# Five shifted copies for VectorE's exponential, column strips for full matmuls, and packed heads, in a fused attention and MLP kernel

## The chip, the cores and the metric

The kernel runs on one core of a Trainium2 chip. Its time is the device time of one launch in microseconds (us). Five engines matter here, named as in the profile: PE (TensorE, matmuls; PEld is its weight load), DVE (VectorE), ACT (ScalarE), POOL (GpSimd) and SP (SyncE, which issues most DMAs). Before the change the median of 3 runs is 805.33 us (805.23 to 805.93).

## The reference, cut to what matters

One input x (2048 tokens by 512, bfloat16) goes through attention with 32 heads of width 16 and through an MLP with two layer norms, two gelus and four weight matrices. A gate for each token mixes the two.

```python
qkv = x @ wqkv                                     # 32 heads, Dh = 16
scores = einsum("bhqd,bhkd->bhqk", q, k) * Dh**-0.5
a = (softmax(scores) @ v) @ wo
h = gelu(layernorm(x) @ w1)                        # quarters of h shifted along the tokens
x1 = x + shifted(h) @ w2
b = x1 + gelu(layernorm(x1) @ w3) @ w4             # w3: 512 x 1792
g = sigmoid((x * gate_w).sum(-1))
out = g * a + (1 - g) * b
```

The softmax needs 32 x 2048 x 2048 exponentials. They are the bulk of the work, and the two engines that make them are ACT and DVE.

## The kernel before

**Units and blocks.** A unit is one chunk of 512 queries (`c`) with four heads (`u`); there are 32 units, worked on one after the other. A unit has 64 blocks: 16 key tiles of 128 (`kt`) by 4 heads (`j`). One block is a score matmul (line 709) that writes 128 keys x 512 queries to PSUM, the exponential, and an attend matmul (line 960) that adds V times the exponentials to the unit's accumulator `acc`. V carries a column of ones, so the sum of the exponentials comes along. The query tile `qT` has two slots: a mask leaves alternate groups of 16 rows at zero in each, so that a head of width 16 fills a row group of 32. Four heads sit in the four row groups of PE and are scored side by side, and the four attend matmuls of one key tile sit in four column groups side by side.

**Two makers of exponentials.** Scores come in slots. A slot has two or three blocks in a `stage` tile, which ACT turns into `pt` with one Exp (line 947). In many slots the third block goes to a tile `dsc` instead, which DVE reads. Four such blocks, of four heads, make a quad. DVE works with the bits of bfloat16 as integers: `dump` (line 873, once for each block) scales the score into exponent and mantissa bits in int16, and four operations over the whole quad (`mantissa` 883, `square` 888, `power` 893, `later` 898) make three terms whose sum approximates the exponential. PE adds each term to `acc` with attend matmuls of its own, so a quad costs PE three attend groups of four.

**The other work.** Projections, MLP matmuls, the gates' products and output tiles are generators (`proj`, `w2_tile`, `w4_tile`, `out_tile`, ...) cut into pieces that go through `bmm` (line 223), one 128 x 128 x 512 matmul at a time, between the scores. A gelu needs another function table on ACT; `gelu_slot` (line 713) then puts gelu matmuls through the score slots, in five places of the run. Where nothing is to be done, `fill` (line 1254) issues a matmul of zeros.

**What sets the order.** The whole program is laid out by a planner inside the kernel when it is built. It holds a time for each engine and an estimated cost for each operation, and picks the next instruction by rank and due time; `RULES` gives each unit its own limits, among them how many blocks DVE may take. Its costs include `MM` (one matmul), `TURN` (what PE loses between kinds of matmul) and the `at[...]` entries, which say when a tile is ready. On the chip the engines run that fixed order and wait for each other by semaphores. SP's queue is in order too: for each unit it copies the sums of exponentials out of `acc` (line 1036), writes their reciprocals to DRAM (1044) and reads them back spread out (1045).

**What the change touches besides.** `q_proj` (line 260) fills both slots of `qT` by one DVE multiplication with `mask` over 128 x 1024. `scale` in `finish_unit` (1048) writes one padded tile `oT` per unit, with 16 of every 32 rows in use; `out_tile` (493) multiplies eight of them per output tile with `wo_pad`. `wants_whole` (643) decides whether a slot gives a block to DVE.

Of the kernel before, what the change touches and what calls it, by code (L numbers as in the profile page):

```python
# [26 lines left out]
SHIFT = 127.0 * 128.0 + 128.0 * log2(0.60404289)  # L27
QUARTER = 32.0 - 3.0 * 128.0
LOWEST = 128.0 - QUARTER


@with_exitstack
def kernel(
# [13 lines left out]
    nc = tc.nc  # L47
# [8 lines left out]
    OB = 8  # L56
# [25 lines left out]
    qpool = ctx.enter_context(tc.tile_pool(name="qpool", bufs=2))  # L82
# [15 lines left out]
    wo_pad = const.tile([P, NU, D], BF16, name="wo_pad")  # L98
# [50 lines left out]
    nc.sync.dma_start(out=gw[:], in_=gate_w.rearrange("(kt p) -> p kt", p=P))  # L149
    for j in range(4):  # L150
        src = A_wo.rearrange("(G j a d) n -> j a d G n", j=4, a=2, d=DH)[j]
        for a in range(2):
            nc.sync.dma_start(
                out=wo_pad[32 * j + 1:32 * j + 1 + DH, :, :].rearrange("d (G a) n -> a d G n", a=2)[a],
                in_=src[a])
# [4 lines left out]
    USUAL = {"NEED": 34, "AHEAD": 16, "HURRY": 14, "DLIM": 1.8, "MANY": 5, "PTS": 4, "CHAINS": 3}  # L160
    RULES = {1: {"NEED": 26, "HURRY": 0, "MANY": 5, "PTS": 6, "CHAINS": 3}, 2: {"NEED": 26, "HURRY": 0, "DLIM": 1.5, "MANY": 4, "PTS": 5}, 4: {"AHEAD": 16, "HURRY": 8}, 6: {"AHEAD": 6, "HURRY": 0, "DLIM": 2.1, "MANY": 4, "CHAINS": 4}, 7: {"MANY": 3, "PTS": 6}, 8: {"NEED": 26, "HURRY": 18, "CHAINS": 3}, 9: {"NEED": 36, "HURRY": 8, "DLIM": 2.1, "MANY": 3, "CHAINS": 5}, 10: {"DLIM": 1.2, "MANY": 5, "CHAINS": 4}, 12: {"NEED": 26, "HURRY": 18, "MANY": 2}, 13: {"HURRY": 8, "PTS": 5}, 14: {"NEED": 28, "AHEAD": 16, "HURRY": 24, "CHAINS": 5}, 15: {"AHEAD": 10, "MANY": 2, "PTS": 5}, 16: {"NEED": 28, "AHEAD": 16, "DLIM": 1.8, "MANY": 2}, 18: {"NEED": 30, "AHEAD": 6, "HURRY": 0, "MANY": 5}, 19: {"NEED": 32, "DLIM": 1.5}, 20: {"AHEAD": 8, "DLIM": 2.1, "MANY": 4, "PTS": 3, "CHAINS": 4}, 21: {"NEED": 32, "AHEAD": 16, "HURRY": 8, "PTS": 5}, 22: {"AHEAD": 8, "HURRY": 18, "MANY": 3, "PTS": 5}, 23: {"NEED": 30, "AHEAD": 12, "HURRY": 14, "DLIM": 2.1, "CHAINS": 4}, 24: {"NEED": 34, "AHEAD": 8, "MANY": 4, "PTS": 5}, 27: {"AHEAD": 10, "DLIM": 1.8, "CHAINS": 4}, 28: {"NEED": 26, "DLIM": 1.5, "MANY": 4}, 29: {"AHEAD": 10, "DLIM": 1.5, "MANY": 5, "CHAINS": 3}, 30: {"NEED": 28, "AHEAD": 10, "DLIM": 1.5, "MANY": 4}, 31: {"NEED": 32, "HURRY": 18, "MANY": 5, "PTS": 6, "CHAINS": 5}}
    MM = 0.2235
    TURN = 0.09
    PE_OUT = 0.43
    WARM = 8
    EARLY = 34
    DUNIT = 1
    MAXD = 16
# [4 lines left out]
    CREDIT = 0.45  # L173
    LATER = 0.4
    GELU, WTWO = 1.0, 1.6
    MOST = 12.0
# [4 lines left out]
    SLACK = 0.3  # L181
    AGE = 2.0
    ARANK = 3
    TANH = 1.5
# [3 lines left out]
    state = {"n": 0, "gen": 0, "young": True, "mm": 0, "kind": "", "t": 0.0, "piece": 0.0,  # L188
# [30 lines left out]

    def bmm(*args, **kwargs):  # L220
        state["mm"] += 1
        state["piece"] += MM
        nc.tensor.matmul(*args, **kwargs)  # L223
# [34 lines left out]
    qTs = {}  # L258

    def q_proj(c, G):  # L260
# [4 lines left out]
        def fn(end):  # L265
            qT = qpool.tile([P, 2, CH], BF16, tag="qT", name="qT")
            qTs[(c, G)] = qT
            nc.vector.tensor_tensor(out=qT[:], in0=ps[:].unsqueeze(1).to_broadcast([P, 2, CH]),
                                    in1=mask[:].unsqueeze(2).to_broadcast([P, 2, CH]), op=ALU.mult)
            at["q", c, G] = end  # L270
# [102 lines left out]
    def gates(c):  # L373
# [3 lines left out]
        for j in range(4):  # L377
# [5 lines left out]
            if j < 3:  # L383
                yield 0.3
# [980 lines left out]
```

## Time and profile before

| | |
|---|---|
| time, median of 3 (range) | 805.33 us (805.23 to 805.93) |
| the profiled execution's span | 803.7 us |
| ACT, PE, DVE busy, share of the span | 98%, 96%, 95% |
| Exp on ACT | 695 instructions, 738.1 us busy |
| score matmuls for ACT, for DVE | 1644, 428 |
| granted TensorE clock | 0.997 |

The profile lists no time of its own execution apart from the span. In it, "xN" is the number of instructions of a group; behind the bar stand the busy time, the mean duration of one, and the engine's idle time just before them with what ended it. Durations of neighbouring instructions overlap by some tens of nanoseconds, so the pitch from start to start is shorter than the duration.

### The profile page before, as it was taken

What the parts mean: (1) busy time and instruction counts of PE and PEld (TensorE: products, weight loads), DVE (VectorE), ACT (ScalarE), POOL (GpSimd) and SP (SyncE); (2) the same over time, 40 slices, a digit from 0 to 9 for tenths busy, and PEclk for the clock granted to TensorE, in tenths of its full rate; (3) what the DMA queues carried; (4) which work ended last, traced back from release to release, by engine and by line L of the source; (5) the groups of instructions that cost most, each with busy time, mean ns of one, the idle gap of its engine ahead of it and who ended that gap; (6) DMA issues with size and microseconds to landing.
All of it is one profiled execution on the core that took longest, in us unless ns stands there. A gap on an engine that the chain in (4) does not pass through costs nothing.

```text
span 803.7 us, 15774 instructions
## 1 busy us (share of the span) xinstructions
PE 773.4 (96%) x6332; PEld 245.8 (31%) x6332; DVE 760.8 (95%) x1237; ACT 787.6 (98%) x734; POOL 19.6 (2%) x46
## 2 busy tenths in 40 slices
PE   9999999999999999999999999999999999999997
PEld 3333333332322323232222233222233233322223
DVE  5799999999889999999999997999999999999995
ACT  6999999999999999999999999999999999999996
POOL 4100000000000000010000000000000000000000
PEclk9999999999999999999999999999999999999998
DMA  8700031230100033001000001001001000000000
GB/s 201 179 15 15 16 67 28 41 42 15 42 1 15 15 106 42 15 1 41 15 14 26 18 15 41 15 3 42 13 14 41 15 6 12 21 21 29 15 15 27
DMA packets 48176, 26.41 MB, mean 33 GB/s; under 512 B 34664, under 2 KB 43624, under 8 KB 48104
## 3 DMA queue, kind: packets, MB, share of 16 engines
q1 hardware_dynamic: 47144, 24.90, 13.0%
q8 instruction: 49, 0.80, 0.4%
q10 hardware_dynamic: 960, 0.52, 0.2%
q14 instruction: 23, 0.19, 0.1%
HBM read 17.04 MB, written 2.35 MB: 24 GB/s over the span
## 4 chain that ended last, share of the span: by engine, by line
ACT 59%; issue 21%; PE 17%; DVE 2%; DVEq 0%; ACTq 0%
ACT pt L947 54%; PE stage L709 5%; PE acc L960 4%; PE ps L223 3%; ACT g2T L925 2%; ACT g2T L928 1%; DVE st L311 1%; ACT L925 1%; PE ps_y L223 1%; PE acc L1259 1%; ACT hT L925 1%; PE ps_v L281 1%; PE ps_k L223 1%; PE warm L1177 0%; PE spare L1262 0%
## 5 line engine op out<-in xcount | busy, mean ns | idle before, releaser
L947 ACT ACTIVATE pt<-stage 128x1024 bf16<-128x1024 f32 (+1 forms) x695 | 738.1, 1236 | 2.6 <-PE stage L709 1.2
L709 PE MATMUL stage<-qT,kT 32*128 32x512 bf16 (+2 forms) x1644 | 270.9, 379 | 22.1 <-ACT pt L947 10.8
L873 DVE TENSOR_SCALAR quad<-dsc 128x512 int16<-128x512 f32 x320 | 213.2, 684 | 13.7 <-PE dsc L709 11.8
L709 PE MATMUL dsc<-qT,kT 32*128 32x512 bf16 x428 | 164.5, 384 | 0.0
L960 PE MATMUL acc<-pt,vp 128*17 128x512 bf16 (+3 forms) x1644 | 157.1, 380 | 1.1 <-ACT pt L947 0.8
L709 PEld LDWEIGHTS <-kT 32*128 32x128 bf16 x2072 | 83.5, 91 | 237.1 <-issue 203.8
L960 PEld LDWEIGHTS <-vp 128*17 128x17 bf16 (+1 forms) x2928 | 60.3, 88 | 131.4 <-issue 119.4
L960 PE MATMUL acc<-quad,vp 128*17 128x512 bf16 x884 | 82.7, 382 | 0.3
L1259 PE MATMUL acc<-wq,zero 128*128 128x512 bf16 x216 | 75.9, 387 | 0.0
L223 PE MATMUL ps<-w,g2T 128*128 128x512 bf16 x224 | 68.4, 384 | 0.8 <-DVE x_sb L433 0.8
L898 DVE TENSOR_SCALAR quad<-quad 128x2048 int16<-128x2048 int16 x80 | 54.2, 679 | 0.3
L223 PE MATMUL ps_y<-xnT,w 128*128 128x512 bf16 x176 | 54.1, 384 | 0.1
L873 DVE TENSOR_SCALAR xT<-dsc 128x512 int16<-128x512 f32 x60 | 40.0, 684 | 0.7 <-PE dsc L709 0.4
L888 DVE TENSOR_TENSOR quad<-quad,quad 128x2048 bf16<-128x2048 bf16 x30 | 36.4, 1213 | 0.3
L883 DVE TENSOR_SCALAR quad<-quad 128x2048 int16<-128x2048 int16 x50 | 34.2, 683 | 0.1
L893 DVE TENSOR_SCALAR quad<-quad 128x2048 int16<-128x2048 int16 x50 | 34.1, 682 | 0.1
L873 DVE TENSOR_SCALAR more<-dsc 128x512 int16<-128x512 f32 x48 | 32.2, 686 | 0.9 <-PE dsc L709 0.2
L1259 PEld LDWEIGHTS <-zero 128*128 128x128 bf16 x216 | 19.1, 96 | 44.8 <-issue 41.6
L223 PEld LDWEIGHTS <-g2T 128*128 128x128 bf16 x224 | 16.9, 97 | 33.1 <-issue 27.5
L723 PE MATMUL stage<-xnT,w 128*128 128x512 bf16 x112 | 25.0, 379 | 0.1
L960 PE MATMUL acc<-more,vp 128*17 128x512 bf16 x248 | 24.3, 382 | 0.0
L1031 DVE COPY accsb<-acc 128x512 f32<-128x512 f32 x31 | 21.2, 684 | 1.6 <-PE acc L960 1.3
(145 smaller groups left out, 682.0 us busy)
## 6 DMA issues: line engine op xcount, KB each, us to landing
bcs<-rec_d SPq DMA_DIRECT2D x31, 256.0 KB
w<-in_B_w_dram SPq DMA_DIRECT2D x2, 1792.0 KB
out_dram<-ot SPq DMA_DIRECT2D x15, 128.0 KB
x_sb<-in_A_x_dram SPq DMA_DIRECT2D x14, 128.0 KB
w<-in_B_w_dram SPq DMA_DIRECT2D x2, 512.0 KB
wkv<-in_A_wqkv_dram SPq DMA_DIRECT2D x1, 512.0 KB
wo_pad<-in_A_wo_dram SPq DMA_DIRECT2D x8, 64.0 KB
xnT<-xn SPq DMA_TRANSPOSE x32
```

Of the source, the lines that this page charges most:

```text
L223: nc.tensor.matmul(*args, **kwargs)
L709: nc.tensor.matmul(out, lhsT=kT[G][32 * j:32 * j + 32, cc, o:o + P], rhs=qTs[(c, G)][32 * j:32 * j + 32, a, lo:hi], start=True, stop=True, ...
L723: nc.tensor.matmul(stages[k][:, i * CH:(i + 1) * CH], lhsT=w[:, kt, m * P:(m + 1) * P], rhs=rhs[:, kt, :], start=(kt == 0), stop=(kt == KT ...
L873: nc.vector.tensor_scalar(out=bits[:, r, :], in0=dsc[:], scalar1=SHIFT, scalar2=LOWEST, op0=ALU.add, op1=ALU.max)
L883: nc.vector.tensor_scalar(out=tiles["once"], in0=bits, scalar1=0x7F, scalar2=0x3F00, op0=ALU.bitwise_and, op1=ALU.bitwise_or)
L888: nc.vector.tensor_tensor(out=tiles["twice"].bitcast(BF16), in0=bits.bitcast(BF16), in1=tiles["once"].bitcast(BF16), op=ALU.mult)
L893: nc.vector.tensor_scalar(out=tiles["once"], in0=bits, scalar1=0x7F80, scalar2=None, op0=ALU.bitwise_and)
L898: nc.vector.tensor_scalar(out=bits, in0=bits, scalar1=QUARTER, scalar2=None, op0=ALU.add)
L925: nc.scalar.activation(out=part, in_=part, func=ACT.Gelu_apprx_tanh)
L947: nc.scalar.activation(out=pt[:, 0:w], in_=stages.pop(k)[:, 0:w], func=ACT.Exp, scale=LN2 / 128.0)
L960: nc.tensor.matmul(accs[n][32 * j:32 * j + M, lo:hi], lhsT=lhsT, rhs=p, start=(kt == 0), stop=(kt == NT - 1), skip_group_check=True, tile_ ...
L1259: nc.tensor.matmul(acc[:], lhsT=zero[:], rhs=wq[:, 0, :], start=False, stop=False, skip_group_check=True)
```

## The change

- **Exponential on DVE.** A quad keeps its four dumps. Instead of three terms out of four operations, DVE makes four copies of the bits, each with a constant added (`STEPS`), and PE sums the five terms. Three more buffers of this kind and freed tiles (`more`, `xT`) hold them.
- **Column strips.** `bmm`, `v_proj`, `gelu_slot` and `fill` issue each full matmul as four of 32 columns of weights, in the four column groups that the attends use. The planner charges `TURN` only between these and the scores. The zero matmuls in `gates` go.
- **Packed heads.** `scale` still writes a padded tile; four DMAs per unit then copy its rows into a tile without gaps that takes two units, so an output tile needs four products with `wo_all` instead of eight. The last two units keep the padded way.
- **Queries by DMA.** From the third query tile on, DVE scales 128 x 512 once, and eight DMAs of 16 rows put the rows into the two slots. The planner takes them as landed 3.5 us later.
- **Slots for DVE alone.** Before the first and after the last gelu slot of a group, `lone_slot` may score up to three blocks that only DVE reads.
- **The planner.** New costs, and `RULES` is set anew for all units.

```diff
-SHIFT = 127.0 * 128.0 + 128.0 * log2(0.60404289)
-QUARTER = 32.0 - 3.0 * 128.0
+STEPS = (-32.0, -57.0, -99.0, -82.0)
+SHIFT = 127.0 * 128.0 - 128.0 * log2(3.95352827)
...
+    wo_rows = A_wo.rearrange("(G j a d) n -> j a d G n", j=4, a=2, d=DH)
     for j in range(4):
         for a in range(2):
+            o = 64 * a + DH * j
+            nc.sync.dma_start(out=wo_all[o:o + DH, :, :], in_=wo_rows[j][a])
...
-    MM = 0.2235
-    TURN = 0.09
+    MM = 0.212
+    TURN = 0.102
+    NARROW = ("full", "attend")
...
+    def strips(out, lhsT, rhs, **kwargs):
+        for j in range(0, P, 32):
+            nc.tensor.matmul(out[j:j + 32, :], lhsT=lhsT[:, j:j + 32], rhs=rhs, tile_position=(0, j), **kwargs)
+
     def bmm(*args, **kwargs):
         state["mm"] += 1
         state["piece"] += MM
-        nc.tensor.matmul(*args, **kwargs)
+        strips(*args, **kwargs)
...
+            both = qpool.tile([P, CH], BF16, tag="both", name="both")
+            nc.vector.tensor_scalar(out=both[:], in0=ps[:], scalar1=QS, scalar2=None, op0=ALU.mult)
+            for o in range(0, P, DH):
+                nc.sync.dma_start(out=qT[o:o + DH, o // DH % 2, :], in_=both[o:o + DH, :])
+            at["q", c, G] = end + 3.5
...
-            bmm(ps[:, 64:CH], lhsT=zero[:], rhs=wq[:, 0, 64:CH], start=True, stop=True)
...
-        for u in range(units):
-            bmm(aps[:], lhsT=oTs[(c, u)][:, j * P:(j + 1) * P], rhs=wo_pad[:, u, :],
-                start=False, stop=(u == units - 1))
+        for G in range(pairs):
+            bmm(aps[:], lhsT=oPs[(c, G)][:, j * P:(j + 1) * P], rhs=wo_all[:, G, :],
+                start=False, stop=(G == pairs - 1))
...
-            t = max(t, done_exp[k - 2], dumped.get(k - 2, 0.0))
+            t = max(t, done_exp[k - 2] + 0.005, dumped.get(k - 2, 0.0) - 0.12)
...
     def scores(start):
         k = len(slots)
+        first, after = gelus and gelus[0][1], state["after"] and not gelus and not ends
+        state["after"] = False
+        if (first and state["before"] or after) and lone_slot(start):
+            state["before"] = not first
+            return
...
+    def lone_slot(start):
...
+        for i in range(3):
+            if i:
+                mine = wants_whole([], start, True)
+            if not mine:
+                break
+            n, kt, j = mine
...
+            score(st[:, i * CH:(i + 1) * CH], n, 4 * kt + j)
+            whole(k, st[:, i * CH:(i + 1) * CH], n, kt, j, begin + (rows[j] - 1) * MM + PE_OUT)
...
-        def mantissa(end):
-            nc.vector.tensor_scalar(out=tiles["once"], in0=bits, scalar1=0x7F, scalar2=0x3F00,
-                                    op0=ALU.bitwise_and, op1=ALU.bitwise_or)
...
-        def square(end):
-            nc.vector.tensor_tensor(out=tiles["twice"].bitcast(BF16), in0=bits.bitcast(BF16), in1=tiles["once"].bitcast(BF16), op=ALU.mult)
...
-        def later(end):
-            nc.vector.tensor_scalar(out=bits, in0=bits, scalar1=QUARTER, scalar2=None, op0=ALU.add)
+        def shifted(end, i):
...
+            base = (0, 0, 0, 1)[i]
...
+            nc.vector.tensor_scalar(out=tiles[to], in0=tiles[base], scalar1=STEPS[i] - (STEPS[0] if base else 0.0), scalar2=None, op0=ALU.add)
...
+            produce(n, kt, heads, tiles[to], end, i == 3, used(to))
...
         def scale(end):
...
+            for j in range(4):
+                nc.sync.dma_start(out=oPs[(c, G)][64 * a + DH * j:64 * a + DH * j + DH, :], in_=oT[32 * j + 1:32 * j + 1 + DH, :])
+            at["o", c, u] = end + 3.0
```

More of the change, by code (lines that the diff above doesn't have):

```diff
@@ L258 @@
     qTs = {}
+    qbufs = [const.tile([P, 2, CH], BF16, name=f"qT{i}") for i in range(2)]
     def q_proj(c, G):
@@ L641, in remaining, with wants_whole @@
         return 4 * NT - place["m"] - sum(4 * kt + j >= place["m"] for kt, j in taken[n])
-    def wants_whole(blocks, now):
+    def wants_whole(blocks, now, alone=False):
         k = len(slots)
-        if k < EARLY or k - quad["last"] < SPACE:
+        if k < EARLY or k - quad["last"] < SPACE and not alone:
             return None
@@ L985, in attend @@
     def attend(start, source):
-        begin = start + (TURN if state["kind"] != "attend" else 0.0)
+        begin = start + (TURN if state["kind"] not in NARROW else 0.0)
         free["pe"] = begin + MM
```

233 lines of the change are left out of this document (152 added, 81 removed).

## The prediction

> **What bounds the kernel now.** I read the page's first part for the load of each engine, then the windows for where an engine rests, then the groups by line and shape, and the timeline for the pitch from one instruction to the next.
>
> ```profile
> PE 773.4 (96%) x6332; PEld 245.8 (31%) x6332; DVE 760.8 (95%) x1237; ACT 787.6 (98%) x734; POOL 19.6 (2%) x46
> ACT 59%; issue 21%; PE 17%; DVE 2%; DVEq 0%; ACTq 0%
> ```
>
> ```profile
> 0.00:50.00 50.00, 47.71 (x331) 17.62 (x331) 35.86 (x87) 43.20 (x48) 13.02 (x41) 1.00 0.63 153
> 100.00:200.00 100.00, 96.32 (x826) 30.14 (x823) 99.16 (x159) 99.89 (x93) 0.00 (x0) 1.00 0.23 39
> 200.00:300.00 100.00, 94.46 (x786) 30.72 (x783) 93.59 (x152) 99.94 (x94) 1.96 (x1) 1.00 0.12 36
> 400.00:500.00 100.00, 96.98 (x783) 30.00 (x781) 94.08 (x146) 99.89 (x92) 0.00 (x0) 1.00 0.08 23
> 700.00:804.00 104.00, 96.83 (x839) 30.66 (x837) 93.58 (x148) 95.78 (x90) 1.26 (x1) 0.98 0.07 21
> ```
>
> In the windows the columns behind the length are PE, PEld, DVE, ACT and POOL. From 100 us on ACT is busy 99.9% until the last window, and the chain that ends last runs mostly over it: a microsecond taken from ACT is a microsecond, as long as PE and DVE keep up. DVE is nearly as full. Its 42.9 us of rest (803.7 - 760.8) lie at the start (14), at the end (10), and 6 each in two windows with a gelu. PE looks full too, but its matmuls overlap and part of them multiply zeros, so its load has to be counted from pitches.
>
> **ACT.**
>
> ```profile
> L947 ACT ACTIVATE pt<-stage 128x1024 bf16<-128x1024 f32 (+1 forms) x695 | 738.1, 1236 | 2.6 <-PE stage L709 1.2 <-PE dsc L709 0.2 <-ACT pt L947 0.2
> L947 ACT ACTIVATE pt<-stage 128x1024 bf16<-128x1024 f32 x465 | 441.7, 1095 | 1.9 <-PE stage L709 1.2 <-PE dsc L709 0.2 <-ACT pt L947 0.2
> L947 ACT ACTIVATE pt<-stage 128x1536 bf16<-128x1536 f32 x230 | 321.5, 1519 | 0.7
> ```
>
> The shapes differ by one block, their means by 424 ns. The 695 instructions hold 465 x 2 + 230 x 3 = 1620 blocks, 686.9 us at 424 ns; the other 51.2 of 738.1 us are 74 ns for each instruction, small waits included. Counted in the changed program, ACT has 485 instructions of two blocks and 202 of three: 1576 blocks in 687 instructions. 1576 x 0.424 + 687 x 0.074 = 719 us, **19.2 us less**. Gelus and table loads are the same in number. The 44 blocks go to DVE (118 quads for 107).
>
> **DVE.**
>
> ```profile
> L873 DVE TENSOR_SCALAR quad<-dsc 128x512 int16<-128x512 f32 x320 | 213.2, 684 | 13.7 <-PE dsc L709 11.8
> L888 DVE TENSOR_TENSOR quad<-quad,quad 128x2048 bf16<-128x2048 bf16 x30 | 36.4, 1213 | 0.3
> L898 DVE TENSOR_SCALAR quad<-quad 128x2048 int16<-128x2048 int16 x80 | 54.2, 679 | 0.3
> L268 DVE TENSOR_TENSOR qT<-ps_q,mask 128x1024 bf16<-128x1024 f32 x15 | 18.2, 1215 | 0.3 <-PE ps_q L223 0.3
> ```
>
> ```profile
> 304.23 1.22 DVE L888 TENSOR_TENSOR quad<-quad,more 128x2048 bf16<-128x2048 bf16 x1
> 305.36 1.28 DVE L873 TENSOR_SCALAR quad<-dsc 128x512 int16<-128x512 f32 x2
> 306.56 0.68 DVE L1031 COPY accsb<-acc 128x512 f32<-128x512 f32 x1
> 307.15 0.68 DVE L893 TENSOR_SCALAR more<-quad 128x2048 int16<-128x2048 int16 x1
> 307.75 0.41 DVE L331 TENSOR_SCALAR xn<-x_sb,mv,rstd 128x512 bf16<-128x512 bf16 x1
> ```
>
> In the timeline the first number is the start. A dump that lasts 684 ns is followed 0.60 us later, an integer operation over a quad too (307.15 to 307.75), `square` 1.13 us later. A quad costs DVE 4 x 0.60 + 3 x 0.60 + 1.13 = 5.33 us before, and 4 x 0.60 + 4 x 0.60 = 4.80 after: a copy is the same kind of instruction as `later` in L898, an added constant over 128x2048 int16. 107 x 5.33 = 570.3, 118 x 4.80 = 566.4: 3.9 us less. 14 query tiles shrink from 1215 ns to a 128x512 operation like the dump (684), 7.4 less. Together **11.3 us less**, for 44 blocks more. Its rest may then be 42.9 - 19.2 + 11.3 = 35 us; the lone slots are put where it rested at a gelu.
>
> **PE.**
>
> ```profile
> 302.14 0.39 PE L1259 MATMUL acc<-wq,zero 128*128 128x512 bf16 x1
> 302.46 0.39 PE L960 MATMUL acc<-quad,vp 128*17 128x512 bf16 x4
> 302.79 0.39 PE L1259 MATMUL acc<-wq,zero 128*128 128x512 bf16 x1
> 304.13 0.39 PE L709 MATMUL stage<-qT,kT 32*128 32x512 bf16 x2
> 304.45 0.39 PE L960 MATMUL acc<-pt,vp 128*17 128x512 bf16 x4
> 304.77 0.39 PE L1259 MATMUL acc<-wq,zero 128*128 128x512 bf16 x1
> ```
>
> ```profile
> 214.87 3.61 PE L723 MATMUL stage<-xnT,w 128*128 128x512 bf16 x16
> 486.79 0.61 PE L960 MATMUL acc<-quad,vp 128*17 128x512 bf16 x8
> 487.23 0.39 PE L960 MATMUL acc<-more,vp 128*17 128x512 bf16 x4
> 487.44 0.39 PE L960 MATMUL acc<-quad,vp 128*17 128x512 bf16 x4
> 487.66 0.39 PE L960 MATMUL acc<-xT,vp 128*17 128x512 bf16 x4
> 487.88 0.39 PE L960 MATMUL acc<-quad,vp 128*17 128x512 bf16 x4
> 488.09 0.60 PE L960 MATMUL acc<-pt,vp 128*17 128x512 bf16 x8
> L1259 PE MATMUL acc<-wq,zero 128*128 128x512 bf16 x216 | 75.9, 387 | 0.0
> L960 PEld LDWEIGHTS <-vp 128*17 128x17 bf16 (+1 forms) x2928 | 60.3, 88 | 131.4 <-issue 119.4
> ```
>
> A change of kind costs 0.32 us from start to start (302.14 to 302.46), the next matmul of the same kind 0.216 (16 in 3.61, the last lasting 0.39). Four attends in four column groups together also take 0.216: eight groups from 486.79 on, 32 matmuls, at an even pitch. A strip differs from an attend in its 32 columns for 17 and in one shared moving operand; I take 0.216 for four. That strips and attends follow each other without a change of kind no row shows; the bounds are 0.216 and 0.32, and I take 0.216, since both are 128 rows by 32 columns and attends change weights and data at that pitch.
>
> Counted in both programs, without the zeros: the five terms add 118 x 5 - 107 x 3 = 269 groups, attends of `pt` lose 11, output tiles 60: 198 more at 0.216, +42.8 us. Changes of kind fall from 1566 to 1237, at 0.106: -34.9. PE's necessary work rises by **8 us**, from about 687 to 695. The zeros fall from 240 (72 us with their changes) to 175 (50). In all PE's order holds 745 us for 759. It is tight, but it fits into 785.
>
> One thing works against it. The new planner constants say 0.212 and 0.314 where the rows say 0.216 and 0.32: over 2786 groups and 1350 changes the order is laid out 16 us too fast for PE. Where PE has zeros to do, that is lost on nobody; where it has not, ACT waits. Between 0 and 16 us; I take 2.5, near zero, because ACT rested 0.1% with a PE load as high.
>
> **Queries and heads by DMA.**
>
> ```profile
> 22.07 4.33 SPq L153 DMA_DIRECT2D wo_pad<-in_A_wo_dram  x8
> 114.86 5.58 SPq L344 DMA_TRANSPOSE xnT<-xn  x4
> SPq L1045 <- DMA rec_d<-rec: 33.1, 31, 1.5
> ```
>
> Eight DMAs of 16 rows keep SP for 4.33 us, 0.54 each, and a small DMA is awaited 33.1 / 31 = 1.07 us after its issue. A query tile's heads thus land 1.6 to 5.4 us after DVE, where the plan counts on 3.5; PE, in order, stands still if a late head is read at once. In the changed program each of the 14 tiles is read one to five Exp instructions after its DMAs are issued (twelve once), and each score waits for its own head's DMA alone. A late last head costs up to 1.9 us, less the slot that is already scored for ACT, and the last is one of four: I take 0.07 for each tile, 1 us; the bounds are 0 and 14 x 1.9 = 27. The copies of packed heads are read an output tile later and cost nothing as long as outputs are not urgent (on the path: up to 1 us a chunk). SP's extra 224 issues of 0.54 us stay far below the span.
>
> Sum: 803.7 - 19.2 + 2.5 + 1 = 788.0 us of span; the median of runs stands 1.6 above the span (805.33 to 803.7), which I keep: **789.6**.
>
> **The rivals.**
>
> *DVE or PE holds ACT back* (main rival): nothing of DVE's rest is recovered, and the span falls by its 11.3 us alone, or PE's 16 us of optimism come through in half. 803.7 - 11.3 + 2 + 1.6 = 796. For: all three engines are full together, and PE has less to leave out. Against: the rest at gelus, which the lone slots address.
>
> *More than ACT's work*: 74 ns per Exp hold small waits; better costs in the planner take some 12 us of 51 away, and the span falls to 776, the time to 778. For: it was laid out with PE's pitch too slow before. Against: PE's pitch is now too fast.
>
> *Slower, late queries*: DMAs queue behind four transposes (5.58 us) or a copy of sums, heads land 7 us late, and PE stands still at each of the 14 tiles. It decides from 19.2 / 14 = 1.4 us a tile; at 1.9 each, 803.7 - 19.2 + 27 + 1.6 = 813. Against: the order puts these DMAs at a unit's beginning.
>
> *Slower, strips are not as quick as one full matmul*: if each group of four leaves one weight load of 88 ns open, 1075 groups add 95 us to PE's 745, and the time is 840 or more; it decides from about 37 ns a group. Against: the run of 32 attends above. The Trainium skill speaks for this rival: "TensorEngine Tiling (Array Packing)", section "Restrictions and Gotchas", says that column tiling excludes the fast weight load. This case's trace disagrees that it costs time, with 0.216 us for four attends. Its page "TensorE: Matmul & The Clock Gate", section "Measured speedup vs the span model", gives 2.38x for three column tiles of 512; by that, as an estimate, a packed group takes 1.26 times a single one, 60 us more for 1075 groups, and the time would be above 800. The attends' pitch speaks against that too.
>
> **How the numbers follow.** Forecast (784 to 794) 0.55; DVE or PE holds back (794 to 803) 0.2; more than ACT's work 0.1; late queries 0.09, most of it slower; slow strips 0.04; the rest, no change, 0.02. The range takes the forecast, the holding back and most of the better case: 779 to 803. A measurement of this kernel tells 0.2%, 1.6 us, from no change. Faster 0.86, same 0.02, slower 0.12.
>
> **What would show it.** Right: 687 Exp with a busy time near 719 us and ACT at 99.9% in the windows; the copies near 680 ns; strips in groups of four 0.216 us apart, and no gap between strips and attends; little time waited for `qT`. Wrong: PE waiting on DMAs of `qT` over a microsecond at a time; a pitch of strips over 0.25 us; Exp waiting for `stage` by tens of microseconds.

## The result and the profile after

The changed kernel takes 832.65 us (median of 4 runs, 831.79 to 833.99) where the kernel before takes 805.43 beside it: a ratio of 1.0338, 95% interval 1.0321 to 1.0355. It is 3.4% slower; 789.6 us had been forecast, 2% faster.

From the page of the profile after, its span, its engines, the granted clock in 40 slices and the chain that ended last:

```profile
span 831.5 us, 24527 instructions
...
PE 782.9 (94%) x10463; PEld 264.9 (32%) x10464; DVE 751.3 (90%) x1325; ACT 774.6 (93%) x726; POOL 15.8 (2%) x46
...
PEclk9999999999999997997999999999999999989999
...
PE 39%; ACT 32%; DVE 13%; issue 11%; DMA 3%; SPq 1%; DVEq 0%; ACTq 0%
```

ACT's work did shrink (787.6 to 774.6 us), but it rests 57 us where it rested 16. Before, the chain that ended last ran over ACT for 59%; now it runs over PE for 39% and over ACT for 32%, and DMAs are on it. The windows (length, PE, PEld, DVE, ACT, POOL, granted clock, DMA share) show where:

```profile
300.00:400.00 100.00, 88.73 (x1073) 27.15 (x1067) 81.93 (x151) 85.87 (x76) 3.12 (x3) 0.88 0.20 46
400.00:500.00 100.00, 97.12 (x1333) 32.01 (x1330) 95.76 (x163) 96.86 (x90) 0.00 (x0) 1.00 0.08 24
...
315.00:330.00 15.00, 11.11 (x101) 2.62 (x105) 7.34 (x13) 7.58 (x7) 0.00 (x0) 0.66 0.20 36
```

Before, ACT was 99.9% busy from 400 to 500 us, now 96.9%: many small waits. From 300 to 400 some large waits come on top, and there TensorE's clock is at 0.88, in the worst 15 us at 0.66. The groups by line (Exp on ACT, dumps and copies on DVE) and the waits (total, times, longest):

```profile
L1038 ACT ACTIVATE pt<-stage 128x1024 bf16<-128x1024 f32 (+1 forms) x687 | 725.0, 1202 | 40.0 <-PE dsc L730 24.0 <-PE stage L730 13.9 <-ACT pt L1038 0.3
...
L929 DVE TENSOR_SCALAR quad<-dsc 128x512 int16<-128x512 f32 x325 | 215.7, 685 | 18.4 <-PE dsc L730 16.8 <-PE stage L730 0.3
...
L966 DVE TENSOR_SCALAR quad<-quad 128x2048 int16<-128x2048 int16 x259 | 171.9, 681 | 8.5 <-PE acc L1051 7.8 <-DVE quad L966 0.5
```

```profile
ACT pt L1038 <- PE dsc L730: 24.0, 23, 5.3
...
ACT pt L1038 <- PE stage L730: 13.9, 20, 2.1
...
DVE oT L1142 <- DMA bcs<-rec_d: 10.1, 3, 4.1
PE ps_y L232 <- DMA xnT<-xn: 4.7, 1, 4.7
...
PE dsc L730 <- DMA qT<-both: 3.7, 2, 3.1
...
DVE rec L1133 <- DMA den<-accsb: 3.4, 3, 1.8
```

Exp idled 2.6 us before and 40.0 now, always for scores. In most of the long waits a DMA stands behind the late scores: the read-back of the reciprocals (`bcs`), the transposed activations (`xnT`) or the query copies themselves, for which PE waited 3.7 us, the least of the three.

For the comparisons below I take each Exp's distance to the next ACT instruction less 904 ns (two blocks) or 1330 (three), the distance in an unbroken row, and add up: 13.7 us before, 57.9 after. Of the 57.9, 20.6 lie in six waits over 1.5 us, 27.0 in 45 waits of 0.25 to 1.5, 10.2 in smaller ones; before, the first sort was absent and the second was 6.3. That closes the account: 831.5 - 803.7 = 27.8 = -19.2 (fewer blocks) + 44.2 (waits) + 2.8 (all else).

A large wait, in the timeline (start, length, engine, line; what it waited for in brackets):

```profile
715.55 5.50 SPq L290 DMA_DIRECT2D qT<-both  x8
...
721.15 0.53 SPq L1134 DMA_DIRECT2D rec_d<-rec  x1
...
722.77 0.58 SPq L1135 DMA_DIRECT2D bcs<-rec_d  x1
...
727.93 0.69 DVE L1142 TENSOR_TENSOR oT<-accsb,bcs 128x512 bf16<-128x512 f32 x1 [3.93 <-DMA bcs<-rec_d]
...
729.28 0.58 PE L730 MATMUL dsc<-qT,kT 32*128 32x512 bf16 x1 [3.44 <-DVE quad L929]
...
731.04 1.02 ACT L1038 ACTIVATE pt<-stage 128x1024 bf16<-128x1024 f32 x1 [3.94 <-PE dsc L730]
```

Eight query copies keep SP for 5.5 us. Here nobody waits for the queries; but the reciprocals' write stands behind them in the queue, then the read-back. DVE in its fixed order waits 3.93 us in `scale` with its dumps behind that, PE waits for a dump to give `dsc` back, ACT waits for PE.

At 189 us it is the query copies themselves that come late, behind four transposes and a copy of sums:

```profile
182.12 5.57 SPq L366 DMA_TRANSPOSE xnT<-xn  x4
...
188.51 4.95 SPq L290 DMA_DIRECT2D qT<-both  x8
...
191.53 0.58 PE L730 MATMUL dsc<-qT,kT 32*128 32x512 bf16 x1 [3.07 <-DMA qT<-both]
...
195.23 1.02 ACT L1038 ACTIVATE pt<-stage 128x1024 bf16<-128x1024 f32 x1 [4.95 <-PE dsc L730]
```

The clock records show TensorE at 0.5 around such places: 6.8 us from 727 us on, and 3.4, 3.4, 10.2 and 13.7 us at 191, 212, 317 and 372 us, 37.5 us together; before, there is none except at the end. All are about multiples of 3.41 us. At four of the five PE stood still for 3.07 to 4.73 us. In the stretches at 317, 372 and 727 us Exp waits about 8 us more, beyond the wait that came first. The Trainium skill, "TensorE: Matmul & The Clock Gate", Part 1, gives half rate after an idle window of about 3.4 us. The lengths agree with such a window, but the place at 212 us does not: in the 3.41 us ahead of it PE is busy for 2.57, partly with the gates' one-column products, and its longest stand is 0.63 us.

The place at 317 us holds another collision, the load of `w4` (1.8 MB) just ahead of four transposes:

```profile
305.75 0.40 SPq L486 DMA_DIRECT2D w<-in_B_w_dram  x1
...
306.19 10.35 SPq L366 DMA_TRANSPOSE xnT<-xn  x4
...
318.37 1.05 PE L232 MATMUL ps_y<-xnT,w 128*32 128x512 bf16 x8 [4.73 <-DMA xnT<-xn]
...
320.05 1.02 ACT L1038 ACTIVATE pt<-stage 128x1024 bf16<-128x1024 f32 x1 [5.35 <-PE dsc L730]
```

And a wait of the middle sort, with no DMA near it:

```profile
655.94 0.39 PE L730 MATMUL stage<-qT,kT 32*128 32x512 bf16 x2
655.95 0.39 PE L730 MATMUL dsc<-qT,kT 32*128 32x512 bf16 x1
...
656.26 0.39 PE L1051 MATMUL acc<-more,vp 128*17 128x512 bf16 x4
...
656.49 0.60 PE L1051 MATMUL acc<-quad,vp 128*17 128x512 bf16 x8
...
657.78 0.39 PE L1051 MATMUL acc<-quad,vp 128*17 128x512 bf16 x4
...
658.10 0.39 PE L730 MATMUL stage<-qT,kT 32*128 32x512 bf16 x2
...
658.59 2.37 ACT L1038 ACTIVATE pt<-stage 128x1024 bf16<-128x1024 f32 x2 [0.97 <-PE dsc L730]
```

Eight groups of term attends in a row lie between two score slots, 2.16 us from score to score, where ACT needs 0.90 for two blocks: it waits 0.97. Counted in the traces, five or more such groups stand between two scores 5 times before and 25 times after.

### The profile page after: what moved, and what is told of

Same layout as the page of the kernel before. It is cut to its first block, busy times and chain, and to the rows that moved or that the text cites. A ratio compares the mean times of both kernels' runs of the same rounds, so it can differ in the third digit from the quotient of the medians.

```text
span 831.5 us, 24527 instructions
## 1 busy us (share of the span) xinstructions
PE 782.9 (94%) x10463; PEld 264.9 (32%) x10464; DVE 751.3 (90%) x1325; ACT 774.6 (93%) x726; POOL 15.8 (2%) x46
## 4 chain that ended last, share of the span: by engine, by line
PE 39%; ACT 32%; DVE 13%; issue 11%; DMA 3%; SPq 1%; DVEq 0%; ACTq 0%
ACT pt L1038 31%; PE acc L1051 14%; PE stage L730 10%; DVE quad L929 4%; DVE quad L966 3%; PE ps_y L232 3%; PE ps L232 3%; PE stage L232 2%; PE acc L232 2%; DMA bcs<-rec_d 1%; PE ps_o L232 1%; SPq L366 1%; PE ps_q L232 1%; PE ps_k L232 1%; DVE xT L966 1%
## 5 line engine op out<-in xcount | busy, mean ns | idle before, releaser
L1038 ACT ACTIVATE pt<-stage 128x1024 bf16<-128x1024 f32 (+1 forms) x687 | 725.0, 1202 | 40.0 <-PE dsc L730 24.0
L730 PE MATMUL stage<-qT,kT 32*128 32x512 bf16 (+1 forms) x1624 | 272.6, 385 | 27.2 <-ACT pt L1038 19.0
L929 DVE TENSOR_SCALAR quad<-dsc 128x512 int16<-128x512 f32 x325 | 215.7, 685 | 18.4 <-PE dsc L730 16.8
L966 DVE TENSOR_SCALAR quad<-quad 128x2048 int16<-128x2048 int16 x259 | 171.9, 681 | 8.5 <-PE acc L1051 7.8
L1051 PE MATMUL acc<-pt,vp 128*17 128x512 bf16 (+2 forms) x1600 | 157.6, 384 | 1.2 <-DVE accsb L1121 0.6
L1051 PE MATMUL acc<-quad,vp 128*17 128x512 bf16 x1604 | 138.3, 386 | 1.1 <-DVE quad L966 1.0
L1051 PEld LDWEIGHTS <-vp 128*17 128x17 bf16 (+1 forms) x3960 | 89.2, 90 | 150.1 <-issue 110.0
L232 PE MATMUL ps<-w,g2T 128*32 128x512 bf16 x896 | 71.1, 385 | 0.0
L232 PE MATMUL acc<-wq,zero 128*32 128x512 bf16 x680 | 63.1, 400 | 0.0
L232 PE MATMUL ps_y<-xnT,w 128*32 128x512 bf16 x704 | 55.8, 393 | 4.7 <-DMA xnT<-xn 4.7
L232 PEld LDWEIGHTS <-w 128*32 128x32 bf16 x1152 | 28.8, 96 | 39.4 <-issue 16.8
L1051 PE MATMUL acc<-more,vp 128*17 128x512 bf16 x400 | 39.1, 386 | 0.2 <-DVE more L966 0.2
L1051 PE MATMUL acc<-xT,vp 128*17 128x512 bf16 x356 | 34.6, 389 | 0.1
```

The lines of the kernel that those rows point to most:

```text
L232: nc.tensor.matmul(out[j:j + 32, :], lhsT=lhsT[:, j:j + 32], rhs=rhs, tile_position=(0, j), **kwargs)
L730: nc.tensor.matmul(out, lhsT=kT[G][32 * j:32 * j + 32, cc, o:o + P], rhs=qTs[(c, G)][32 * j:32 * j + 32, a, lo:hi], start=True, stop=True, ...
L929: nc.vector.tensor_scalar(out=bits[:, r, :], in0=dsc[:], scalar1=SHIFT, scalar2=LOWEST, op0=ALU.add, op1=ALU.max)
L966: nc.vector.tensor_scalar(out=tiles[to], in0=tiles[base], scalar1=STEPS[i] - (STEPS[0] if base else 0.0), scalar2=None, op0=ALU.add)
L1038: nc.scalar.activation(out=pt[:, 0:w], in_=stages.pop(k)[:, 0:w], func=ACT.Exp, scale=LN2 / 128.0)
L1051: nc.tensor.matmul(accs[n][32 * j:32 * j + M, lo:hi], lhsT=lhsT, rhs=p, start=(kt == 0), stop=(kt == NT - 1), skip_group_check=True, tile_ ...
```

## The experiments

All were run three rounds or more beside the kernel before, which took 804.8 to 806.8 us. Unless an edit says otherwise, the order of the instructions on PE, DVE and ACT is that of the kernel after. "Waits" is the sum explained above (13.7 before, 57.9 after).

### Is it the strips, or the zeros left out?

`before_strips`: the kernel before, with strips for all full matmuls.

```diff
+    def strips(out, lhsT, rhs, **kwargs):
+        for j in range(0, P, 32):
+            nc.tensor.matmul(out[j:j + 32, :], lhsT=lhsT[:, j:j + 32], rhs=rhs, tile_position=(0, j), **kwargs)
...
-        nc.tensor.matmul(*args, **kwargs)
+        strips(*args, **kwargs)
```

> The kernel before with each full matmul as four column strips and nothing else changed; its planner still counts a turn between strips and attends. Theory S: strips cost nothing and PE is not the bound, 803-807. Rival: strips take longer than one matmul or cost in weight loads, 812 or more.

805.4 us, ratio 0.9992 [0.998, 1.0004]. Strips cost nothing; the rival of slow strips falls.

`gate_zeros`: the zeros among the gates' light products put back.

```diff
+            strips(ps[:, 64:CH], lhsT=zero[:], rhs=wq[:, 0, 64:CH], start=True, stop=True)
             state["piece"] += 0.2
```

> The changed kernel with the 16 zero matmuls (as strips) put back among the gates' one-column products, and nothing else moved. Theory S with the clock: the halving of the clock at 211.6 us, which stands behind light gate products and not behind a wait, goes away, and with it 2 to 4 us: 828-831. Theory P: PE gets 3.5 us more work, 832-836.

831.78 us, ratio 1.0325 [1.0301, 1.0348], between the two ranges. The half clock at 212 us went, another came at 248, and the waits stayed at 57.0. The light products are not the cause of the lost time.

`no_fill`: the 175 zero groups of `fill` left out.

```diff
-            strips(acc[:], lhsT=zero[:], rhs=wq[:, 0, :], start=False, stop=False, skip_group_check=True)
...
-            strips(spare[:], lhsT=zero[:], rhs=wq[:, 0, :], start=True, stop=True)
+            pass
```

> The changed kernel without its 175 groups of zero matmuls, everything else in the same order: PE has 45 us less to do. Theory P: the time falls by 10 us or more, to 822 or below. Theory S: 826-836, since the long waits are for DMAs; where PE has less to do its clock may halve more often.

833.21 us, ratio 1.0342 [1.0318, 1.0365]. PE's busy time fell from 782.9 to 748.1 us and the time did not move: PE's load over the whole run is not the bound. The half clock within the run rose from 37.5 to 58.0 us, so the zeros do serve the clock, and a few microseconds of gain may be hidden behind that: the waits of 0.25 to 1.5 us fell to 24.1, the long ones rose to 24.6.

### Is it SP's queue?

`pool_queue`: query copies and head copies issued by GpSimd.

```diff
-                nc.sync.dma_start(out=qT[o:o + DH, o // DH % 2, :], in_=both[o:o + DH, :])
+                nc.gpsimd.dma_start(out=qT[o:o + DH, o // DH % 2, :], in_=both[o:o + DH, :])
...
-                nc.sync.dma_start(out=oPs[(c, G)][64 * a + DH * j:64 * a + DH * j + DH, :], in_=oT[32 * j + 1:32 * j + 1 + DH, :])
+                nc.gpsimd.dma_start(out=oPs[(c, G)][64 * a + DH * j:64 * a + DH * j + DH, :], in_=oT[32 * j + 1:32 * j + 1 + DH, :])
```

> The changed kernel with the copies of queries and of packed heads (232 small DMAs) issued from GpSimd's queue instead of SP's; the order on PE, VectorE and ScalarE is the same, instruction for instruction. Theory S (SP's queue is late against the plan; each long wait also halves the TensorE clock): SP's DMAs of sums and reciprocals are no longer queued behind copies, VectorE's waits for bcs fall from 10.1 us to under 2, and the time falls from 832 to 805-820, less if GpSimd's own queue brings the queries late. Theory P (PE's order is laid out too fast and PE is the bound): SP has no part in it, 828-834.

823.21 us, ratio 1.0215 [1.02, 1.0231]; waits 39.0. It is faster than the kernel after, but by less than theory S said, and one wait of 3.8 us for `bcs` stays. `chain_pool`: the other way round, the reciprocals' write and read-back on GpSimd.

```diff
-            nc.sync.dma_start(out=rd.rearrange("j (b e) -> (j b) e", e=DH), in_=rec[:])
-            nc.sync.dma_start(out=bcs[:], in_=rd.unsqueeze(1).to_broadcast([4, 32, CH]))
+            nc.gpsimd.dma_start(out=rd.rearrange("j (b e) -> (j b) e", e=DH), in_=rec[:])
+            nc.gpsimd.dma_start(out=bcs[:], in_=rd.unsqueeze(1).to_broadcast([4, 32, CH]))
```

> The changed kernel with the write of reciprocals and their read-back (62 DMAs) issued from GpSimd's queue, the 232 copies left on SP; order on the other engines as it was. Theory S: the read-back no longer stands behind eight query copies or four transposes, VectorE's 10.1 us of waits for bcs fall under 3, the late queries at 191 us stay: 818-826. Theory P: 830-834.

823.30 us, ratio 1.0209 [1.0191, 1.0227]; waits 46.8. The time is the one expected, but DVE's waits for `bcs` fell only to 7.3 us, not under 3. `w4_pool` moves only the load of `w4` to GpSimd:

```diff
-        nc.sync.dma_start(out=w4[:], in_=wview(B_w4))
+        nc.gpsimd.dma_start(out=w4[:], in_=wview(B_w4))
```

> The changed kernel with one DMA moved: the 1.8 MB load of w4 is issued from GpSimd's queue, so that the four transposes issued right behind it (10.35 us on SP, the first 6.07) no longer follow it in SP's queue. Order on PE, VectorE and ScalarE as in the changed kernel. Theory S: PE's wait of 4.7 us for xnT at 313 us goes, and the 10 us of half clock behind it: 822-827. Theory P (PE's order too fast and too full): 830-834.

833.18 us, ratio 1.0332 [1.0316, 1.0349], a miss: the wait for `xnT` is 5.4 us. With the load issued 2 us ahead of them on GpSimd's queue the transposes took 11.26 us. `spread` moves the chain, the heads, `w4` and the copies of the slot read first, and leaves the other query copies on SP:

```diff
+            for a in range(2):
+                for o in range(a * DH, P, 2 * DH):
+                    (nc.sync if a else nc.gpsimd).dma_start(out=qT[o:o + DH, a, :], in_=both[o:o + DH, :])
```

> The changed kernel with SP's load spread: the four copies of a query tile that are read first, the packed heads, the reciprocals' chain and the load of w4 on GpSimd's queue, the other four query copies on SP; order on the other engines as it was. Theory S: all long waits and nearly all half clock go, what stays are waits of 0.5 to 1.3 us behind runs of attends at the units' starts: 800-812. Theory P: 815 or more.

823.11 us, ratio 1.022 [1.0196, 1.0244], a miss; waits 39.1. `w4_after` is `spread` with the load on SP behind the transposes:

```diff
-        nc.gpsimd.dma_start(out=w4[:], in_=wview(B_w4))
         res = []
         yield from norm_T(1, 0, res)
+        nc.sync.dma_start(out=w4[:], in_=wview(B_w4))
```

> The kernel with SP's load spread (first-read query copies, heads and the reciprocals' chain on GpSimd's queue), with the load of w4 on SP behind the four transposes instead of before or beside them; order on the other engines as it was. Theory S (transposes were slow because they run beside 1.8 MB): the wait of 5 us for xnT goes, 823 falls to 815-819. Otherwise 821-825.

823.82 us, ratio 1.0231 [1.0199, 1.0263]: the wait for `xnT` is gone and the time stays. The edit had little left to mend: in `spread` the load was issued at 299.0 us, after all four transposes (from 294.5 us on, 5.2 us), and the wait was only 1.2 us. `one_copy` does not move copies, it takes them away: one DMA for eight and one for four, 44 on SP in place of 232.

```diff
-            for o in range(0, P, DH):
-                nc.sync.dma_start(out=qT[o:o + DH, o // DH % 2, :], in_=both[o:o + DH, :])
+            nc.sync.dma_start(out=qT[:, 0, :], in_=both[:])
...
-            for j in range(4):
-                nc.sync.dma_start(out=oPs[(c, G)][64 * a + DH * j:64 * a + DH * j + DH, :], in_=oT[32 * j + 1:32 * j + 1 + DH, :])
+            nc.sync.dma_start(out=oPs[(c, G)][64 * a:64 * a + 64, :], in_=oT[0:64, :])
```

> The changed kernel with one DMA for each query tile instead of eight (all 128 rows into the first slot, the second slot left stale) and one for each unit's heads instead of four (64 rows unpacked): 44 copies on SP instead of 232, the computation of queries and heads left wrong; order on PE, VectorE and ScalarE as it was. Theory S (SP's queue): as with the copies on GpSimd's queue or better, 812-822. If the copies' latency and not their number on SP mattered: 828 or more.

813.64 us, ratio 1.0098 [1.0083, 1.0114], 19.0 us under the kernel after; waits 39.0. From its waits:

```profile
ACT pt L1037 <- PE stage L729: 12.4, 17, 2.4
...
ACT pt L1037 <- PE dsc L729: 10.0, 15, 3.4
...
DVE oT L1141 <- DMA bcs<-rec_d: 4.3, 1, 4.3
...
PE ps_y L232 <- DMA xnT<-xn: 2.8, 1, 2.8
```

Why did moving the same copies give only 9.4? `pool_queue` has the same waits as `one_copy` (39.0) and is 9.6 us slower. `masked` and `masked_sp` answer it: no query is copied, the mask multiply of before makes both slots on DVE, and `w4` is loaded behind the transposes. `masked` copies heads on GpSimd, `masked_sp` on SP.

```diff
-            both = qpool.tile([P, CH], BF16, tag="both", name="both")
-            nc.vector.tensor_scalar(out=both[:], in0=ps[:], scalar1=QS, scalar2=None, op0=ALU.mult)
-            for o in range(0, P, DH):
-                nc.sync.dma_start(out=qT[o:o + DH, o // DH % 2, :], in_=both[o:o + DH, :])
+            nc.vector.tensor_tensor(out=qT[:], in0=ps[:].unsqueeze(1).to_broadcast([P, 2, CH]),
+                                    in1=mask[:].unsqueeze(2).to_broadcast([P, 2, CH]), op=ALU.mult)
```

> The whole computation again: the order of TensorE, VectorE and ScalarE's work is that of the kernel after, but no query is copied (VectorE writes both of its halves by the mask multiply of before, 1215 ns in place of 683, 14 times: 7.4 us more of VectorE), the 120 head copies are issued on GpSimd's queue, and the load of w4 is issued behind the four transposes. SP keeps the reciprocals' chains and the transposes alone. Theory (it is the 16-row copies ahead of other things in one queue that cost the 19 us, wherever SP's 0.63 us apiece stand): about as one_copy or less, with VectorE's 7.4 us at places where a third of it at most is waited for: 808 to 815 us; the wait of the multiply for bcs in total under 6 us, and that of dsc for qT gone. Rival (the 19 us came from what one_copy left out or from any change of the moment at which things land, since every other mend of the queue stayed at 823): 820 to 828. Second rival (VectorE at 91% busy has no room, and 0.53 us each lies on the path): one_copy's 813.6 + 7.4 = 821, with the waits of pt for dsc up by that.

> The kernel masked with the 120 head copies back on SP's queue; nothing else differs. In masked the last output is issued at 808.3 us of the profiled run, and the span ends only at 818.3, where it ends 3 us behind the last output in the kernel after: GpSimd's last instruction there is a drain of 11.2 us. Theory (a GpSimd queue that carried the small copies has to be emptied at the end, 7 us that belong to none of the work, and it hid half of what the copies cost in every kernel that moved them): the 7 us go, the last output comes 0 to 3 us later since four head copies of 0.6 us stand ahead of some sums, span 811 to 814, median 812.5 to 815.5. Rival (masked is slower than one_copy because VectorE has 7.4 us more to do): it stays at 818 to 822 with the last output near 815.

819.51 us, ratio 1.0163 [1.0134, 1.0192], waits 36.0, for `masked`, between what its theory and its rivals gave; 815.06, ratio 1.0105 [1.0074, 1.0136], waits 40.1, for `masked_sp`, as its theory had it. The span of each, with the last row of its timeline, first of `masked`:

```profile
span 818.3 us, 24421 instructions
...
808.05 0.93 SPq L1245 DMA_DIRECT2D out_dram<-ot  x2
```

then of `masked_sp`:

```profile
span 813.1 us, 24362 instructions
...
809.87 0.90 SPq L1245 DMA_DIRECT2D out_dram<-ot  x2
```

`masked` issues its last output 1.8 us earlier and ends 5.2 us later. Near the end GpSimd has a drain instruction. It takes 11.2 us in `masked` and 1.4 in `masked_sp`, as in the kernel after; it took 10.5 to 11.0 in `pool_queue`, `spread` and `w4_after`, and 3.0 in `chain_pool`. So 6 to 7 us of the times of `masked`, `pool_queue`, `spread` and `w4_after` are spent in GpSimd's drain, behind all other work. By the last output's issue (828.3 us in the kernel after), `pool_queue` gained 16.0 us, `spread` 17.9, `one_copy` 19.2, `masked` 20.2 and `masked_sp` 18.4. The gain is much the same whether the query copies move to another queue, become fewer or go altogether. `masked_sp` keeps the 120 head copies on SP and has nearly all of it, so the 112 query copies are the larger part.

### Is it the five terms?

`three_terms` leaves two of each quad's five attend groups out, 236 groups.

```diff
-            produce(n, kt, heads, tiles[to], end, i == 3, used(to))
+            produce(n, kt, heads, tiles[to], end, None if i < 2 else i == 3, used(to))
...
-                for r, j in enumerate(heads):
+                for r, j in enumerate(heads if ending is not None else ()):
```

> The changed kernel with two of the five terms of each quad left out on PE (944 attend matmuls, 236 groups, 51 us of PE; VectorE still makes the copies); order otherwise as it was. Theory B (runs of up to nine groups of terms between two slots of scores let ScalarE run dry by 0.3 to 1.3 us at a time): ScalarE's middle waits fall by 8 to 15 us and the time to 815-824, although leaving out 45 us of zero matmuls brought nothing. Theory without B: as without the zeros, 830-835.

825.51 us, ratio 1.0244 [1.0217, 1.0271]: 7.1 us less, just short of theory B's range. The waits of 0.25 to 1.5 us fall from 27.0 to 17.1, as theory B said, the long ones stay (24.3). Five or more groups stand between two scores 3 times now instead of 25. `no_fill` had about as little for PE to do (748.1 us busy; 746.8 here) with the runs as they were, and gained nothing. That points to the place of the terms, between two scores, more than to PE's load. `all_three` joins `one_copy`, the later `w4` and `three_terms`:

> One copy for eight and for four, w4 behind the transposes, and two of five terms left out on PE, all in one; order otherwise as in the changed kernel. If SP's queue and the runs of terms are the whole of the loss, ScalarE's waits come to 15 to 22 us, little more than the 13.7 of the kernel before, the clock stays whole, and the time comes to 788-798, which is what the prediction summed. If something else holds it: 805 or more.

800.05 us, ratio 0.9934 [0.9913, 0.9956], waits 23.9 and none over 1.5 us: a little above the first range, and far from 805. The clock's line of its page, and its waits:

```profile
PEclk9999999999999999999999999999999999999999
```

```profile
ACT pt L1037 <- PE stage L729: 5.3, 11, 0.9
...
ACT pt L1037 <- PE dsc L729: 4.3, 8, 0.9
```

A 9 in the clock's line is 90% or more of a slice; the clock records still have three stretches of 3.4 us at 0.5, and no stand of PE near them is over 1 us. `all_three` is the only version below the kernel before, with what `one_copy` and `three_terms` leave out of the computation.

### Can a better order have the gain?

`late_plan` tells the planner of later landings and keeps `RULES`, which were made for the old ones.

```diff
-            at["q", c, G] = end + 3.5
+            at["q", c, G] = end + 9.0
...
-            post("vector", 0 if n >= len(units) - 3 else 3, 0.25, recip, end + 2.3)
+            post("vector", 0 if n >= len(units) - 3 else 3, 0.25, recip, end + 4.5)
```

and likewise the read-back 7.6 to 13, heads 3 to 6, `XPOSE` 9 to 14.

> The changed kernel with the planner told later landings: queries 9.0 us after VectorE instead of 3.5, sums 4.5 for 2.3, reciprocals spread 13.0 for 7.6, packed heads 6.0 for 3.0, transposes 14.0 for 9.0; the planner lays the order out anew, with 460 blocks on VectorE instead of 472. Theory S: PE and VectorE no longer stand in front of late DMAs, the clock stays whole, and the time comes to 793-808. Theory P: PE's order is as dense as before, 820-835.

902.81 us, ratio 1.1204 [1.1187, 1.1221]. The new order is bad in itself (`pt` waits 63.1 us for `acc`), so this tells nothing of landings. `replan` and `replan_runs` therefore start from `masked_sp`, give PE's true costs and search `RULES` anew; they differ in how long a run of term attends may be.

```diff
-    MM = 0.212
-    TURN = 0.102
+    MM = 0.216
+    TURN = 0.106
...
-    RUN = 9.5
+    RUN = 3.5
```

> The whole computation, as masked_sp (queries by the mask multiply, head copies on SP, w4 behind the transposes), but laid out anew: the planner is told 0.216 for a group and 0.106 for a turn, the multiply's 1.23, landings of 7.8 (read-back), 3.8 (heads) and 9.3 us (transposes), and it may put at most 4 term groups between two score slots (RUN 3.5 for 9.5); RULES and USUAL are searched for these costs. VectorE gets 113 quads in place of 118, so ScalarE makes 20 blocks more than after at 0.424 us: Exp busy near 733. Theory (late landings and long runs of terms were what cost the 42 us, not the five terms or the strips): waits of ScalarE back near the kernel before's 13.7 us, no half clock in the midst, time 794 to 804. Rival (an order of five terms always leaves ScalarE waiting, since TensorE has too little room): waits of 30 us and more, 810 to 820.

> As replan, but the runs of term attends may be as long as in the kernel after (RUN 9.5), with RULES and USUAL searched for that. 115 quads. Theory that long runs matter by themselves: 3 to 7 us above replan, through more waits of pt for stage and dsc of 0.25 to 1.5 us. Rival (runs cost only where the order had been laid out for other landings): within 3 us of replan.

816.79 us, ratio 1.0142 [1.0115, 1.0169], waits 32.1, for `replan`; 814.72, ratio 1.0107 [1.0081, 1.0132], waits 27.8, for `replan_runs`. Both miss their theories, and each lies where its rival put it: `replan` at 810 to 820 with waits over 30 us, `replan_runs` within 3 us of `replan`. But in `replan` one wait of 9.9 us stands out, behind a copy of sums that was issued just after `w4`. Its waits of 0.25 to 1.5 us are 15.9 us, those of `replan_runs` 22.3: shorter runs did take small waits away, and the one long wait hides that in the time. (The two orders differ in other things too, since `RULES` was searched for each.) `replan_w4` splits that load:

```diff
-        nc.sync.dma_start(out=w4[:], in_=wview(B_w4))
...
+                if c == 0 and m < 7:
+                    nc.sync.dma_start(out=w4[:, 2 * m:2 * m + 2, :], in_=w4_rows[:, 2 * m:2 * m + 2, :])
```

> The kernel replan with one edit: the load of w4 (1.8 MB) is not issued whole behind the four transposes but in seven parts of 256 KB, one behind each of the next gelu inputs; the order on TensorE, VectorE and ScalarE is the same. In replan a copy of sums of 8 KB stands right behind that load; the reciprocal waited 8.7 us for it, ScalarE 9.9 us, and TensorE ran 13.7 us at half its clock afterwards. Theory (that one event is what replan has left of long waits): its wait goes, the longest left is under 2 us, no half clock in the midst, and the time falls by 10 to 13 us to 803 to 807, level with the kernel before. Rival (the transposes are what the sums' copy waits for, the load only stands beside them): the wait of the reciprocal stays over 4 us, and the time at 811 or more.

812.05 us, ratio 1.0076 [1.0062, 1.0089], waits 29.4. Its timeline there:

```profile
311.15 6.12 SPq L364 DMA_TRANSPOSE xnT<-xn  x4
...
317.38 0.61 SPq L1126 DMA_DIRECT2D den<-accsb  x1
...
319.38 0.25 DVE L1133 RECIPROCAL rec<-den 128x16 f32<-128x16 f32 x1 [3.34 <-DMA den<-accsb]
```

The reciprocal's wait fell from 8.7 to 3.3 us and no further: the rest is the queue behind the transposes, 6.1 us of SP. So 5.4 us of the event was the load and the rest the transposes; neither theory had both. Of the versions with five terms that leave nothing out it is the fastest, and the kernel before stays 0.8% faster.

## Why the prediction was wrong, point by point

**ACT's work: right.** 687 Exp, as counted, at the same distances of 904 and 1330 ns; the 19.2 us are in the account. (Their busy time is 725.0 for 719. An Exp of two blocks lasts 1.02 us alone and 0.90 from start to start in a row, so each wait behind one adds about 0.1 us; some 50 waits over 0.25 us account for the difference.)

**DVE: right in cost.** Dumps at 685 ns and copies at 681, where 684 and 679 were used. DVE's busy time fell by 9.5 us where 11.3 had been summed, and it had rest to spare, as forecast. Where its rest lies mattered more: it waits in order, with the dumps behind the wait. (The five terms are the dumped tile and four copies of it; the title counts all five as copies.)

**Strips: right.** The profile after has sixteen groups of four in 3.64 us, the last lasting 0.39, thus 0.216 us each, and 0.21 us from an attend to a strip, so no change of kind; `before_strips` has 0.9992.

```profile
219.80 3.64 PE L232 MATMUL stage<-xnT,w 128*32 128x512 bf16 x64
...
659.08 0.39 PE L1051 MATMUL acc<-pt,vp 128*17 128x512 bf16 x4
659.29 0.60 PE L232 MATMUL ps_y<-xnT,w 128*32 128x512 bf16 x8
```

**Queries and heads by DMA: the step that failed.** The term was 1 us, with bounds of 0 and 27 from late heads. It measured 19 us (`one_copy`, with the heads), and 18 in `masked_sp`, which also has the later `w4`. That 19 lies within the bounds is luck, since they were made for another wait. The copies were charged only to those who read them: what PE waited for `qT` was 3.7 us in all, though Exp lost 4.95 us behind the one late tile at 189 us. And SP's load was called far below the span, as a total, which is true (its DMA issues sum to about 270 us of 831) and was not the point. SP's queue is in order: eight copies hold it for 4.9 to 6.1 us (0.62 to 0.76 us each, 0.54 had been assumed; 232 copies, 224 had been counted), and the reciprocals' write, the read-back and the copy of sums stand behind them with a wait on DVE at the end. The rival "late queries" (813 us, chance 0.09) named "DMAs queue behind four transposes", which happened at one tile of 14, but not what queues behind the DMAs; it had the right queue, for the most part the wrong waiter, and its time was too low.

**PE: totals right, the step to a stage missing.** PE's busy time rose by 9.5 us (773.4 to 782.9), part of it at half clock, and `no_fill` shows that the total does not bind. But a two-block slot gives PE 0.92 us (2 x 0.424 + 0.074); a score group and two turns take 0.43 of it, so only 0.49 are left, 2.3 groups, those of `pt` among them. Five terms for three make longer runs, and runs of up to nine groups stand between two scores. Leaving two terms out took 7 us away (`three_terms`); together with the later `w4`, behind `one_copy`, 13.6 (813.64 to 800.05). The main rival, "DVE or PE holds ACT back" (796 us, chance 0.2), saw PE as the limit, but as half of 16 us over the whole run and not in single slots. The rival "more than ACT's work" expected small waits to shrink by 12 us; those of 0.25 to 1.5 us grew by 20.7.

**No term for the clock.** At each of the four places where PE stood still for 3 us or more, the clock was halved for 3.4 to 13.7 us, so that a late DMA costs more than its wait: about 8 us of further waits lie in those stretches. Other stretches of 3.4 to 10.2 us came without such a stand (at 212 us here, at 358 us in `masked`, where PE's longest stand is 1.5 us); the runs don't tell what brings those on. The prediction's row of the clock (1.00 nearly throughout) was that of a kernel with next to no waits.

**The planner's lag** (2.5 us, 0 to 16) was not tested by itself. In `replan`, with true costs, ACT still waits 32.1 us.

**What stays open.** Of the 43.1 us between forecast and result, the copies account for 19.0 and the terms with the place of `w4` for 13.6; the other 10.5, from 789.6 to the 800.05 of `all_three`, which even leaves work out, no run explains. `all_three` has 23.9 us of waits and the searched orders 27.8 to 32.1, where the kernel before has 13.7. Most are small waits of Exp for scores. Whether they belong to the five terms, or to orders that were searched less well than that of before, the runs don't tell: with runs limited to four groups, `replan` still has 15.9 us of waits of 0.25 to 1.5 us, before 6.3.

## What to carry to other kernels

A DMA that "nobody waits for" must be priced by its place in its queue: list what is issued behind it on that engine, and who waits in order for that. In a kernel laid out by hand or by a planner, an engine's load has to fit each slot and not only the span: divide what the bounding engine gives per slot by the pitch, and compare it with the longest run the new order puts there. When a move to another queue gives half of what taking the work away gives, look at the end of the trace for what the other queue adds.

## What the runs showed of the hardware that had not been expected

- Eight 16-row copies from SBUF to SBUF hold SP for 4.9 to 6.1 us, 0.62 to 0.76 us each. One copy of all 128 rows, with the same rows in one DMA, holds it for 0.51 (`one_copy`): the number of DMAs counted here, not what they carry.
- Four transposes issued in a row hold SP for 5.1 to 6.1 us, and for 10.35 behind a load of 1.8 MB, 11.26 with that load on GpSimd's queue (`w4_pool`).
- With the 120 copies of packed heads on GpSimd's queue, alone or with others, its drain at the kernel's end was 10.5 to 11.2 us long for 1.4 without, and 6 to 7 us of them lay beyond all other work; with the 62 DMAs of the reciprocals' chain alone it was 3.0.
- Column strips of 32 take over from attends of 17 columns without a gap, four in 0.216 us, as one full matmul does.
- The granted clock fell to half for 3.4 us with PE busy 2.57 of the 3.41 us before (at 212 us).
